# TensorE in source order in the last three blocks, the seven products of a unit in another order, and later transposes of x

## The chip, the cores and the metric

The kernel runs on one core of one Trainium2 chip. The time is that of one execution on the device, in microseconds; before the change the median of seven runs is 352.6 us (351.54 to 353.11).

## The reference

Sliding-window attention with an ALiBi bias, and then a SwiGLU feed-forward block on its result:

```python
B, H, S, D = q.shape                      # 8, 8, 576, 64; window 128
scores = scale * np.matmul(q, k.transpose(0, 1, 3, 2))
bias = slopes[:, None, None] * (-np.abs(rel))[None, :, :]
scores = np.where((rel >= 0) & (rel < window), scores + bias[None], -1000000000.0)
attn = softmax(scores)
attn_out = np.matmul(attn, v)
x = attn_out.transpose(0, 2, 1, 3).reshape(B * S, H * D)      # 4608 x 512
g = x @ w_gate                                                # 512 x 1536
return (g * sigmoid(g) * (x @ w_val)) @ w_out                 # 1536 x 512
```

Input and output are float32.

## The kernel before

Matmuls take float16 operands. Attention is cut into 36 units of 128 query rows. For a unit i, `scores(i)` makes the score products in PSUM (pool `ps_a`, four banks, tag "a"), exponentials on ScalarE and mask products on VectorE; `weighted(i)` (L344 to L347) multiplies by v on TensorE and normalises into the tile x on VectorE; `x_transposed(i)` brings x into xT, the input of the feed-forward block: by four TensorE transposes and a ScalarE copy (L370, L374) up to unit 23, by a transposing DMA on SP's queue (L365) from unit 24 on (`X_DMA_FROM`).

The feed-forward part works on nine blocks n of 512 tokens. Blocks 0 to 5 take each column of w_gate and w_val by plain 512-column matmuls (L396). Blocks 6, 7 and 8 (`gate_val_by_seven`) use Strassen's scheme (Winograd's form): 2 x 2 blocks by seven products in place of eight. A block has six units u; each of the seven products of a unit is four matmuls of 256 columns (L615) into one of three PSUM tiles: X and Y from the four banks of `ps_a`, Z from `ps_f`. Results are chained through these tiles:

- `first` starts X, and ScalarE copies X into Z (L624); `second` accumulates onto Z, then a silu on ScalarE gives s1 (L637).
- `fifth` starts Y, and ScalarE copies it to p5 (L630); `sixth` accumulates onto X, and ScalarE copies that to u2 (L644).
- `third` accumulates onto Y; VectorE adds u2 (v1, L651) and multiplies by s1 into hT (L652).
- `seventh` accumulates onto X; VectorE adds p5 (v2, L658). `fourth` accumulates onto X once more; a silu (L665) and a product on VectorE (L666) finish hT.

So each product that accumulates onto X, Y or Z has to wait for the engine that reads what was there. After the fourth product of units 3, 4 and 5 VectorE makes sums of hT (`sums`, L490 to L493) into the buffers S, of which there is one set.

The output product of a block, hT times w_out, is also done by seven products (`strassen`), once for each t in 0 and 1, so in 14 parts of six 256-column matmuls (L523), which run during the next block: `ffn` puts one part after every third product of `gate_val_by_seven`. These parts read the buffers S of their own block. After block 8 its own 14 parts follow.

What sets the order: the program is a generator for the feed-forward part (`ffn`), which counts steps, and one for attention; `everything` mixes them by a pace (`RATE`, and `ready` for the units that a block needs). This is the source order. Inside `tc.manual_schedule(engines=...)` the named engines issue in source order; that covers the first tiles up to step 8 (`ALONE`). Outside it a planner places the instructions of each engine at build time, the earlier in the source the sooner, but passing over those that by its own estimate of times are not ready. On the chip each engine's order is then fixed.

## Time and profile before

| | |
|---|---|
| median of 7 runs | 352.6 us |
| the profiled execution | 352.34 us |
| its span, first to last instruction | 350.5 us |
| TensorE busy (modelled ends) | 337.9 us, 96% |
| VectorE busy | 276.4 us, 79% |
| ScalarE busy | 205.4 us, 59% |
| GpSimd (loads) busy | 108.2 us, 31% |
| block 6 / 7 / 8 begin (first product) | 251.30 / 277.46 / 306.18 us |

A row of the timeline has the start, the duration, the engine, the line, the operation, the output and the inputs by name, the form and the number of instructions merged into it; in brackets the idle time ahead of it and what ended it. A row of the list of waits has the instruction, what it waited for, the sum, the number of times and the longest. PE is TensorE, PEld its weight loads, DVE VectorE, ACT ScalarE. The tile X of the Strassen units appears as gX, Y as gY, Z as gZ; m_reg, m_c, kT and qT are buffers of the attention part that hold sums of weights and of x in the last blocks.

## The change

From the step at which block 6 begins (198.0) TensorE issues in source order. Within a unit the order of the products, first, fifth, fourth of the unit before, second, sixth, third, seventh, becomes first, seventh of the unit before, fifth, sixth, fourth of the unit before, second, third. The transposes of x of the units 13 to 23 are put later: not right after the unit's own `weighted`, but into the third step of the scores of the second unit after it; the number of finished units that attention reports is one lower meanwhile.

```diff
--- before.py
+++ after.py
@@ -33,6 +33,8 @@
 SILU_AT = 7
 SECOND = 5.5
 RATE = 6.7
+FIXED_FROM = 198.0
+LATE = 13
 
 
 def slot(h):
@@ -645,14 +647,14 @@
             live[u] += (u2,)
 
         def third(u):
-            X, Y, Z, p5, s, u2 = live[u]
+            X, Y, Z, p5, u2, s = live[u]
             product(Y, V2, 2 * u * P, S4)
             v_ = supool.tile([P, 2, 256], FP16, name="v1", tag="uu")
             nc.vector.tensor_add(v_, Y, u2)
             nc.vector.tensor_mul(hT[n][:, 2 * u:2 * u + 2, 0:256], s, v_)
 
         def seventh(u):
-            X, Y, Z, p5, s, u2 = live[u]
+            X, Y, Z, p5, u2, s = live[u]
             product(X, tsum[u][2], 0, S3)
             v_ = supool.tile([P, 2, 256], FP16, name="v2", tag="uu")
             nc.vector.tensor_add(v_, X, p5)
@@ -667,8 +669,8 @@
 
         last_u = NMB // 2
         for u in range(last_u + 1):
-            for step, of in ((first, u), (fifth, u), (fourth, u - 1), (second, u), (sixth, u),
-                             (third, u), (seventh, u)):
+            for step, of in ((first, u), (seventh, u - 1), (fifth, u), (sixth, u), (fourth, u - 1),
+                             (second, u), (third, u)):
                 if 0 <= of < last_u:
                     step(of)
                     if step is fourth and of >= last_u // 2:
@@ -792,19 +794,29 @@
 
     def attention():
 
+        waiting = set()
         transposes_to(need[FIRST])
         for _ in run(scores(FIRST)):
             yield FIRST
         for i in range(FIRST, last + 1):
+            behind = LATE <= i < X_DMA_FROM
             if i < last:
                 transposes_to(need[i + 1])
-                for _ in run(scores(i + 1)):
-                    yield i
+                for n, _ in enumerate(run(scores(i + 1))):
+                    yield i - (i - 1 in waiting)
+                    if n == 2 and i - 1 in waiting:
+                        x_transposed(i - 1)
+                        waiting.discard(i - 1)
             weighted(i)
             yield i
             loads_to(i + 7)
             ahead(i)
             yield i
+            if behind:
+                waiting.add(i)
+                yield i
+                yield i
+                continue
             x_transposed(i)
             yield i
             yield i + 1
@@ -884,7 +896,11 @@
                     nc.scalar.copy(idm2, idm)
                 if at in (1.0, 3.0, 4.0):
                     later_masks(2 * (1, 3, 4).index(at) + 2, 2)
+        fixed = ExitStack()
         for step in steps:
+            if step >= FIXED_FROM and fixed is not None:
+                fixed.enter_context(tc.manual_schedule(engines=ENGINES["pe"]))
+                fixed, held = None, fixed
             if step == MASKS_AT:
                 make_masks()
 
@@ -902,6 +918,7 @@
                 target = base + 32 + SECOND * 8 + (step - 60) * RATE * 8 / 34.5
             while (n_att < target or done < ready[blk]) and att_step():
                 pass
+        held.close()
 
     everything()
 
```

## What I expect

> **What bounds the kernel now.** I read the page first, its busy times and its slices; then the list of waits; then the timeline of TensorE and VectorE over the last three blocks, and the one around the x transposes.

> ```profile
> PE 337.9 (96%) x2983; PEld 218.9 (62%) x2983; DVE 276.4 (79%) x652; ACT 205.4 (59%) x412; POOL 108.2 (31%) x134
> ...
> PEclk9999999999999999999999999999999999999999
> ```

> TensorE is the bound, at full clock throughout. Its 96% is not the measure, since the ends of matmuls are modelled (a 256-column one reads 273 ns); what counts is the distance from start to start. In the timeline a group of four 256-column matmuls is followed by the next after 0.437 us, a group of six after 0.655 us: 109.2 ns each, with nothing between. From the first product of block 6 (251.30 us) to the last matmul's slot (345.85 + 0.655 = 346.50) lie 95.20 us. Three blocks of 42 products of four and 14 parts of six, and 14 more parts at the end, are 3 x 252 + 84 = 840 matmuls, or 91.73 us. So TensorE loses only 3.5 us there, and that is all that an order of these instructions can win.

> The end of block 6 on TensorE:

> ```profile
> 273.97 0.82 PE L523 MATMUL po<-T,S 128*128 128x256 f16 x6
> ...
> 276.59 0.60 PE L615 MATMUL gX<-m_reg,m_c 128*128 128x256 f16 x4
> 277.02 0.60 PE L615 MATMUL gY<-m_reg,wv_sb 128*128 128x256 f16 x4
> 277.46 0.38 PE L615 MATMUL gX<-xT,wg_sb 128*128 128x256 f16 x2
> 277.86 0.60 PE L615 MATMUL gX<-m_reg,m_c 128*128 128x256 f16 x4
> 278.39 0.82 PE L523 MATMUL po<-T,hT 128*128 128x256 f16 x6
> 279.04 0.38 PE L615 MATMUL gX<-xT,wg_sb 128*128 128x256 f16 x2
> 279.26 0.60 PE L615 MATMUL gY<-xT,kT 128*128 128x256 f16 x4
> 279.70 0.82 PE L523 MATMUL po<-wo_sb,hT 128*128 128x256 f16 x6
> 280.59 0.60 PE L615 MATMUL gX<-xT,m_c 128*128 128x256 f16 x4
> ```

> From the second row on this is sixth, third, (half of the next block's first), seventh, a part of the output product, (the rest of that first, the next block's fifth, the next block's first part), fourth. The brackets are 4 + 4 + 6 = 14 matmuls, 1.53 us, pulled ahead of source order; and the fourth still starts 0.24 us after its turn. VectorE in the same stretch:

> ```profile
> 274.57 0.41 DVE L652 TENSOR_TENSOR hT<-s,v 128x512 f16<-128x512 f16 x1
> 274.90 0.42 DVE L490 TENSOR_TENSOR S<-hT 128x512 f16<-128x512 f16 x1
> ...
> 278.25 0.42 DVE L492 TENSOR_TENSOR S<-hT 128x512 f16<-128x512 f16 x1
> 278.58 0.68 DVE L651 TENSOR_TENSOR v<-gY,u 128x512 f16<-128x512 f32 x1
> 279.18 0.42 DVE L493 TENSOR_TENSOR S<-hT,S 128x512 f16<-128x512 f16 x1
> 279.52 0.42 DVE L652 TENSOR_TENSOR hT<-s,v 128x512 f16<-128x512 f16 x1
> 279.85 0.68 DVE L658 TENSOR_TENSOR v<-gX,p 128x512 f16<-128x512 f32 x1
> ```

> It runs without a pause. The sums of h (L490 to L493) write buffers that the output product of the block before still reads, so they start only when the part at 273.97 is through, and then stand ahead of what the last unit needs: its v1 (278.58), hT and v2 (L658). v2 ends at 280.53 and TensorE goes on at 280.59.

> From the waits, and the timeline around unit 15's transposes:

> ```profile
> PEld L370 <- DVE x L347: 10.2, 24, 1.0
> ```

> ```profile
> 118.40 0.59 PE L396 MATMUL pg<-xT,wg_sb 128*128 128x512 f16 x2
> 119.29 0.28 PE L370 MATMUL px<-idm,x 128*128 128x128 f16 x2 [0.30 <-DVE x L347]
> ```

> Two 512-column matmuls take 0.43 us, so the transposes could start at 118.83 and start at 119.29: 0.46 us lost because VectorE had not finished x.

> [...]

> **The change part by part.** No instruction is added or removed; all is order.

> *Order within a unit.* Now sixth to seventh has only third between, and in two units of a block no output part: the copy of X (L644, 583 ns) ends too late, and I count 0.18 us at 263.6, 277.6, 287.6, 292.4, 306.3, 320.9 and 334.9. In the new order five products lie between: gone. Newly close is first to sixth (0.87 us of products, and always one part of 0.655, since a part follows every third product): 1.53 us between them, against copy L624: 0.60 (modelled end of the group) less 0.44, plus 0.04 to 0.1 start, 0.57, 0.06 back = 0.83 to 0.9. Covered with 0.6 us, which also takes a silu (0.6) queued ahead on ScalarE. Seventh to fourth: two products and one part, 1.53 us, against v2: 0.16 + 0.1 + 0.69 + 0.06 = 1.01; 0.5 us spare for VectorE being late, as before. Fifth to third and fourth to the next first are at least as far. So the middle of a block has no wait. The two at 285.2 and 313.7 (0.35 and 0.39 us, fourth of unit 0 behind VectorE's backlog) go too if TensorE has stood still before and VectorE has caught up: worth 0.74.

> *Source order at the end of a block.* The last entries are seventh of unit 5, one part (0.655), fourth of unit 5: the new order does not change this. From the part at 273.97 to that fourth, source order holds three parts and six products, 42 matmuls, 4.59 us: due at 278.56. VectorE's work up to v2 is the same set: the sums start with the same part, at 274.90, and the shift of seventh of unit 4 by 0.44 us is hidden, because v1 and hT of that unit (0.60 + 0.33) run first. So fourth starts at 280.59 again: 2.03 us of standing still where now it is 0.24, 0.18 and a 0.10 bank wait, the rest filled. Blocks 7 and 8 give the same: 302.69 + 4.59 = 307.28 against 309.31, 331.27 + 4.59 = 335.86 against 337.89, 2.03 each. The bounds: at least 0.36 (1.45 us from the seventh's start to v2's release, 1.09 in between) if v2 meets an empty VectorE; 1.0 if three of the 0.33 us operations (a sum or two, hT) fall behind v2; at most about 2.3. I take 2.03, since VectorE was ordered alike in all three blocks and those operations stand earlier in the source. After the last block four parts (2.62 us) cover the sums of its last unit, with some 0.25 us of waits at the end.

> Sum for the blocks: 3 x 2.03 + 0.25 = 6.3 us of loss against 3.5: **+2.8 us** (bounds -2.2 and +3.7).

> *Late x transposes, units 13 to 23.* Each is moved five attention steps on, behind the score products and three exponentials of a later unit; its ScalarE copy moves with it. No DMA moves with it, and SP's transposing DMAs begin at unit 24 as before. Start to start, I count 2.0 us lost ahead of and within these eleven units' transposes, some 1.5 to 1.6 of it waiting for x (0.46, 0.28, 0.20, 0.29 and smaller ones), the rest changes between matmul forms. A delay of some 3 us covers waits of under 0.5. Against it: VectorE is 71 to 91% busy there (14.29 us of the 20 from 105 on, 18.21 of the next 20), so a TensorE that comes earlier may wait at the next product that needs it, and the planner reorders everything behind. Bounds -2.0 and +0.8; I take **-1.2**. The block that reads xT asks for finished units, so attention is only pulled ahead by up to one unit; no engine gets more work.

> Total: 352.34 (this execution; span 350.5 and 1.8 around it) + 2.8 - 1.2 = **354.0 us**. The execution lies 0.3 below the median of 352.6; I make no correction for that. What can't be told from no change is 0.2%, 0.7 us.

> **Rivals.**
> 1. *VectorE takes v2 earlier* (faster). The order of VectorE is planned anew once TensorE is fixed. With X us of standing still at each block's end the total is 3X + 0.25 - 3.5 - 1.2; it turns to a gain below X = 1.5. With three operations behind v2, X = 1.0: 351.0 us; with an empty VectorE, X = 0.36: 349.0. For it: the needed work is only 1.0 us. Against: three identical VectorE orders, with sums that precede v2 in the source.
> 2. *It cancels*: X near 1.5 or late transposes worth the full 2.0: about 352.5 us. For it: many waits on x; against: the 2.03 seen thrice.
> 3. *The late transposes win nothing or cost*: the waits for x return at the next products: 352.34 + 2.8 + 0 to 0.8 = 355.1 to 355.9. For it: VectorE's load. Against: few other TensorE waits on VectorE between units 13 and 23.
> 4. *TensorE isn't held to source order*: then the 14 matmuls still fill, and only the new order of products counts, 352.34 - 1.3 - 1.2 = 349.8. Little speaks for it.

> **Chances.** Forecast (353.3 to 355) 0.44; rival 1 0.19; rival 2 0.20; rival 3 0.14; rival 4 0.03. Slower 0.58, same 0.20, faster 0.22. The forecast's own range is 353.2 to 355.0; the range for 8 in 10 takes in half of rival 1 and most of rival 3: 350.8 to 355.4.

> **What would show it.** Right: at the end of each block seventh, six matmuls of a part, a gap near 2 us ended by v (L658), fourth; no waits of 0.18 on L644; no wait on L347 in units 13 to 23. Wrong: a gap under 1.5 us there, with L658 ahead of sums on VectorE; or new TensorE gaps between 105 and 175 us.

## The result and the profile after

The changed kernel takes 353.95 us (median of 13 runs, 353.08 to 356.65) against 352.49 (34 runs, 351.42 to 353.11) for the kernel before: ratio 1.0063, 95% interval 1.0048 to 1.0079. It is slower by 0.6%. The profiled execution is the one of 353.95 us, with a span of 352.2. (Lines from L35 on are counted two higher than before, and those of `gate_val_by_seven` likewise: L523 is now L525, L615 L617, L658 L660, L370 L372.)

The page of the kernel after, TensorE's work and clock:

```profile
PE 335.8 (95%) x2983; PEld 220.3 (63%) x2983; DVE 277.8 (79%) x652; ACT 206.9 (59%) x412; POOL 108.2 (31%) x134
...
PEclk9999999999999999999999999999999999999989
```

The instructions are as many as before on every engine. What differs is when they run, and, in one slice near the end, TensorE's granted clock, which PEclk gives in tenths of its full speed.

Where block 6 begins, on TensorE (timeline; start, duration, instruction):

```profile
247.36 1.03 PE L398 MATMUL pv<-xT,wv_sb 128*128 128x512 f16 x4
248.22 0.60 PE L617 MATMUL gX<-xT,wg_sb 128*128 128x256 f16 x4
```

That was 251.30 us: 3.1 us were won before the last blocks. From there to the end of the last matmul it took 95.20 us before; now it takes 99.88 (248.22 to 348.10): 4.7 us were lost. The difference of the two spans, 1.6 us, is these two numbers.

The wait of the weight loads for x, from the list of waits, and unit 15's transposes on the timeline:

```profile
PEld L372 <- DVE x L349: 6.3, 14, 1.0
```

```profile
120.54 0.82 PE L525 MATMUL po<-T,S 128*128 128x256 f16 x6
121.19 0.39 PE L372 MATMUL px<-idm,x 128*128 128x128 f16 x4
```

It was 10.2 us in 24 waits. The transposes follow a group of six after 0.65 us, which is exactly its time, and run without a break. Counted from start to start, the eleven units 13 to 23 lose 0.12 us around their transposes, where they lost 2.0.

The end of block 6 on TensorE:

```profile
272.68 0.82 PE L525 MATMUL po<-wo_sb,S 128*128 128x256 f16 x6
273.33 0.60 PE L617 MATMUL gZ<-xT,wg_sb 128*128 128x256 f16 x4
273.77 0.60 PE L617 MATMUL gY<-m_reg,wv_sb 128*128 128x256 f16 x4
274.20 0.60 PE L617 MATMUL gX<-m_reg,m_c 128*128 128x256 f16 x4
275.26 0.82 PE L525 MATMUL po<-T,hT 128*128 128x256 f16 x6 [0.46 <-DVE osb L529]
277.46 0.60 PE L617 MATMUL gX<-xT,m_c 128*128 128x256 f16 x4 [1.39 <-DVE v L660]
```

These are second, third, seventh, an output part and fourth, in source order, with nothing of the next block between. The part starts 1.06 us after the seventh in place of 0.437: 0.62 us lost. The fourth starts 2.20 us after the part in place of 0.655: 1.55 us lost. The bracket names a smaller time, since it counts from the modelled end of the matmul. Blocks 7 and 8 show the same two gaps to within 0.01 us (they end at 304.94 and 307.14, and at 334.61 and 336.81). VectorE beside it:

```profile
274.79 0.42 DVE L529 SCALAR_TENSOR_TENSOR osb<-po,u2s 128x256 f32<-128x256 f32 x1
275.12 0.41 DVE L494 TENSOR_TENSOR S<-hT 128x512 f16<-128x512 f16 x1
275.45 0.69 DVE L653 TENSOR_TENSOR v<-gY,u 128x512 f16<-128x512 f32 x1
276.06 0.41 DVE L495 TENSOR_TENSOR S<-hT,S 128x512 f16<-128x512 f16 x1
276.39 0.42 DVE L654 TENSOR_TENSOR hT<-s,v 128x512 f16<-128x512 f16 x1
276.73 0.68 DVE L660 TENSOR_TENSOR v<-gX,p 128x512 f16<-128x512 f32 x1
```

VectorE's operations come in the order of before. Both gaps end when VectorE is through with something: the first with the read of the output tile at 274.79 (the part writes the same PSUM tile, po), the second with v2, which ends at 277.41.

After the third gap, in block 8, the clock falls (windows; the last three columns are the granted clock, the share of the DMA engines and GB/s), and the matmuls that follow show it:

```profile
333.91:337.32 3.41, 1.57 (x14) 1.11 (x12) 2.85 (x7) 0.45 (x2) 0.00 (x0) 1.00 0.38 148
337.32:340.73 3.41, 3.41 (x18) 2.46 (x17) 1.70 (x4) 1.36 (x3) 0.00 (x0) 0.50 0.02 5
340.73:344.15 3.42, 3.42 (x33) 3.04 (x31) 1.25 (x3) 0.77 (x2) 0.00 (x0) 1.00 0.09 22
```

```profile
337.24 2.68 PE L525 MATMUL po<-wo_sb,hT 128*128 128x256 f16 x12
339.72 1.98 PE L525 MATMUL p<-wo_sb,hT 128*128 128x256 f16 x12
```

Twelve 256-column matmuls now take 2.48 us from start to start, where they took 1.31. From 337.24 to 341.53 the 24 matmuls take 4.29 us in place of 24 x 0.109 = 2.62: 1.7 us. So the 4.7 us are 3 x 2.17 = 6.5 us of gaps and 1.7 of clock, less the 3.5 us of waits that were there before; no other wait of note is left.

## The experiments

The shares of the change are tried alone first, then what makes TensorE stand still, then the clock, then how far the gain goes. Ratios are to the kernel before, run beside it on the same chip.

### Late transposes alone

The changed kernel without the fixed order and with the old order of products:

```diff
-            if step >= FIXED_FROM and fixed is not None:
-                fixed.enter_context(tc.manual_schedule(engines=ENGINES["pe"]))
-                fixed, held = None, fixed
...
-            for step, of in ((first, u), (seventh, u - 1), (fifth, u), (sixth, u), (fourth, u - 1),
-                             (second, u), (third, u)):
+            for step, of in ((first, u), (fifth, u), (fourth, u - 1), (second, u), (sixth, u),
+                             (third, u), (seventh, u)):
```

> The late transposes of x alone; TensorE is left to the planner and the products keep their old order. Theory (the waits for x are the gain, and they don't come back): block 6 begins some 3.1 us earlier, as in the changed kernel (248.2), the last blocks stay at 95.2 us, so about 349.4 us. Rival (the gain before block 6 is lent, not given: the last blocks then wait longer for VectorE): 351 to 352.5 us, with block 6 earlier and a longer rest. Only 1.2 us gained, as I had reckoned: 351.3.

Measured: 350.08 us (6 runs) against 352.35, ratio 0.9943 (0.9926 to 0.9960), so 2.0 us won, 1.4 to 2.6. In its profile block 6 begins at 248.80 and the rest takes 95.19 us, the 95.20 of before; the transposes of units 13 to 23 lose 0.12 us. The gain is kept to the end: the rival of a lent gain falls, and so does my 1.2. The 3.1 us of a single pair of profiles was too much. Up to 105 us, where the first moved transposes lie, TensorE has the same instructions in the same order in both kernels, and yet 0.67 us of the 3.1 were there by 57 us. The kernel before, then the changed one:

```profile
56.42 0.59 PE L450 MATMUL po<-wo_sb,hT 128*128 128x512 f16 x2 [0.89 <-DMA wo_sb<-in_moe_w_out_dram]
56.85 1.02 PE L396 MATMUL pg<-xT,wg_sb 128*128 128x512 f16 x4
```

```profile
55.56 0.59 PE L452 MATMUL po<-wo_sb,hT 128*128 128x512 f16 x2
56.18 1.02 PE L398 MATMUL pg<-xT,wg_sb 128*128 128x512 f16 x4
```

In one execution TensorE stood still for 1.05 us until w_out had been transferred, in the other it lost 0.19 us there. That leaves 2.4 us for the late transposes, and with them alone it is 2.4 as well (251.30 less 248.80, less 0.06 that were there before them). In the four runs below without late transposes, whose order on TensorE up to block 6 is that of before, block 6 begins anywhere from 250.3 to 252.1 us.

### Source order and new order of products, no late transposes

```diff
-LATE = 13
+LATE = 24
```

> TensorE in source order from block 6 on and the new order of products, without the late transposes. Theory (standing still at each block's end): block 6 begins at 251.3, three gaps of 2.1 to 2.2 us in all, 352.5 + 2.9 = 355.4 us, and up to 1.8 us more in executions where the clock is halved after a gap: median 355.4 to 357.2. Rival (source order costs nothing and the late transposes are what costs): 352.5 or less.

Measured: 356.43 us (6 runs, 354.78 to 358.96), ratio 1.0135 (1.0097 to 1.0174). The profile, of the execution of 354.78 us, has the clock whole up to the last matmul and takes 98.20 us from block 6 on: 3.0 more than before. The gaps are 0.62 and 1.55 us in each block. The late transposes are not what costs.

### New order of products alone

The changed kernel without the three lines that enter `manual_schedule`, and with `LATE = 24`.

> The new order of the seven products alone, TensorE left to the planner. Theory (the new order takes the seven waits of 0.18 us on the copy of X away, and the planner still pulls matmuls of the next block ahead of the fourth of unit 5): 352.5 - 1.3 = 351.2 us, no gap over 0.4 us in the last blocks. Rival (the new order by itself makes v2 late): gaps of over 1 us at the blocks' ends, 354 us or more.

Measured: 351.42 us (22 runs), ratio 0.9974 (0.9964 to 0.9984), 0.9 us faster. From block 6 on it takes 94.19 us, 1.0 less than before; no wait on the copy of X is left. I missed one thing: a gap of 0.51 us in each block ahead of the output part, ended by VectorE's read of the output tile. There is none of over 1 us.

### Source order alone

The old order of products, as in the diff of the late transposes alone, with `LATE = 24` and `manual_schedule` kept.

> TensorE in source order from block 6 on with the old order of products, no late transposes. Theory (the block's end is what source order costs, whatever the order of products): the same three gaps of some 2.1 us, and the waits of 0.18 us in units whose sixth and seventh have no output part between: 352.5 + 2.9 + 0.5 to 1.0 = 356 us, up to 1.8 more by the clock. Rival (the new order makes the gap at the end): under 354 us.

Measured: 355.55 us (6 runs, 355.18 to 356.55), ratio 1.0107 (1.0086 to 1.0128). TensorE at the end of block 6:

```profile
276.76 0.60 PE L617 MATMUL gY<-m_reg,wv_sb 128*128 128x256 f16 x4
277.60 0.60 PE L617 MATMUL gX<-m_reg,m_c 128*128 128x256 f16 x4 [0.24 <-ACT u L646]
278.13 0.81 PE L525 MATMUL po<-T,hT 128*128 128x256 f16 x6
280.33 0.60 PE L617 MATMUL gX<-xT,m_c 128*128 128x256 f16 x4 [1.39 <-DVE v L660]
```

The fourth waits 1.55 us as with the new order: the new order does not make that gap. The 0.62 us ahead of the part are only 0.09 here, but TensorE has already waited ahead of the seventh. Ahead of the seventh stands what the new order was to remove, the wait on the copy of X: 0.40 us under source order (277.60 less 276.76 less 0.437), where the planner's filling had left 0.18. It comes twice in a block. From block 6 on it takes 99.01 us, 0.8 more than with the new order.

### The sums of h asked for later

The cause named in the prediction is that VectorE's sums stand ahead of v2. Here they are only asked for later in the source; the planner then puts them behind.

```diff
-                    if step is fourth and of >= last_u // 2:
-                        sums(n, of - last_u // 2)
+                    if step is fourth and of == last_u - 1:
+                        for c in range(3):
+                            sums(n, c)
```

> The changed kernel, with the sums of h of a block asked for only after the fourth of unit 5, so that the planner puts v1 and v2 of unit 5 ahead of four of VectorE's operations. Theory (TensorE stands still because these operations are ahead of v2): v2 some 4 x 0.335 = 1.3 us earlier, the two gaps at each block's end 0.8 us together in place of 2.2, no halved clock, so about 353.3 - 3 x 1.3 = 349.4 us, a little more if the last block's sums are late for the output parts. Rival (TensorE waits for its own chain, sixth to seventh to fourth, and VectorE's queue doesn't matter): gaps as before, 353 to 354 us.

Measured: 349.22 us (6 runs, 348.95 to 349.32), ratio 0.9911 (0.9890 to 0.9931). TensorE, then VectorE, at the end of block 6:

```profile
275.29 0.60 PE L617 MATMUL gX<-m_reg,m_c 128*128 128x256 f16 x4
275.73 0.82 PE L525 MATMUL po<-T,hT 128*128 128x256 f16 x6
277.20 0.60 PE L617 MATMUL gX<-xT,m_c 128*128 128x256 f16 x4 [0.66 <-DVE v L660]
```

```profile
275.54 0.41 DVE L495 TENSOR_TENSOR S<-hT,S 128x512 f16<-128x512 f16 x1
275.87 0.68 DVE L653 TENSOR_TENSOR v<-gY,u 128x512 f16<-128x512 f32 x1
276.47 0.68 DVE L660 TENSOR_TENSOR v<-gX,p 128x512 f16<-128x512 f32 x1
277.07 0.41 DVE L654 TENSOR_TENSOR hT<-s,v 128x512 f16<-128x512 f16 x1
277.40 0.41 DVE L493 TENSOR_TENSOR hT<-hT 128x512 f16<-128x512 f16 x1
```

v2 now follows v1 at once. The gap ahead of the part is gone, and the fourth starts 1.47 us after it in place of 2.20: 0.82 us lost, all in all, in place of 2.17, in each of the three blocks. The 1.35 us are four operations of 0.335, as reckoned. So it is VectorE's queue that holds TensorE. From block 6 on it takes 94.17 us, and the last block's sums are not late for the output parts.

### Something to do in the gap

Six matmuls whose result nobody reads, ahead of the fourth of unit 5 in each block; they are work added, not a part of the computation.

```diff
+                    if step is fourth and of == last_u - 1:
+                        nil = ps_f.tile([P, 512], FP32, name="nil", tag="gv")
+                        for _ in range(6):
+                            nc.tensor.matmul(nil, wg_sb[:, 0, 0:P], wg_sb[:, 0, 0:512], start=True, stop=True)
                     step(of)
```

> The changed kernel with six 512-column matmuls of no use (1.3 us, into a PSUM buffer nobody reads) ahead of the fourth of unit 5 in each block, where TensorE stands still anyway. Theory (the halved clock after some of the gaps comes from TensorE's idleness): the fourth starts at the same time, the clock stays whole in all runs, and all runs lie where the changed kernel's runs of whole clock lie: 353.1 to 353.7 us. Rival (the halving has another cause): runs spread up to 356.6 us as in the changed kernel.

Measured: 352.76 us (14 runs, 351.94 to 353.63), ratio 1.0019 (1.0004 to 1.0033). TensorE at the end of block 6:

```profile
274.44 0.60 PE L617 MATMUL gX<-m_reg,m_c 128*128 128x256 f16 x4
275.50 0.81 PE L525 MATMUL po<-T,hT 128*128 128x256 f16 x6 [0.45 <-DVE osb L529]
276.15 1.46 PE L678 MATMUL nil<-wg_sb 128*128 128x512 f16 x6
277.70 0.60 PE L617 MATMUL gX<-xT,m_c 128*128 128x256 f16 x4
```

From seventh to fourth it is 3.26 us, as in the changed kernel (274.20 to 277.46): the added matmuls cost nothing, as the wait is set by VectorE. No run reaches 353.7 us and none has a mean clock below 0.995; the changed kernel has four runs at 355.5 to 356.7 us, with a mean clock of 0.988 or 0.989. So the halving goes when the gap is filled, and it is worth about 1.2 us of the median (353.95 against 352.76, two series of runs). In the profile of this kernel the last blocks take 98.20 us, which is the 99.88 of the changed kernel less its 1.7 us of halved clock. The runs lie half a microsecond lower than I had written. Two of them have a mean clock of 0.995 (353.28 and 353.63 us); without their traces it can't be said where in the run that was lost, and the kernel before has runs at 0.993 (352.53 us) that are no slower than some of its runs at 1.0 (352.55 to 352.69).

### Late transposes and new order, TensorE left to the planner

The change without its `manual_schedule`.

> The late transposes and the new order of products, TensorE left to the planner: the change without its fixed order. Theory: both gains and no gap: 352.5 - 3.1 - 1.3 = 348.1 us. Rival (order and late transposes gain the same microsecond): 349.4.

Measured: 349.24 us (6 runs, 347.97 to 350.56), ratio 0.9913 (0.9889 to 0.9937). That is more time than I expected, because I had taken the late transposes at the 3.1 us of the profiles; with the 2.0 and 0.9 us that the two edits won alone, 352.36 becomes 349.5. The number is the rival's, but its reason is not: from block 6 on it takes 94.18 us, where late transposes alone have 95.19, so the new order wins its 1.0 us beside them. What the planner does with the end of block 6:

```profile
273.95 0.60 PE L617 MATMUL gX<-m_reg,m_c 128*128 128x256 f16 x4
274.39 0.27 PE L617 MATMUL gX<-xT,wg_sb 128*128 128x256 f16 x1
275.00 0.82 PE L525 MATMUL po<-T,hT 128*128 128x256 f16 x6 [0.34 <-DVE osb L529]
275.65 0.49 PE L617 MATMUL gX<-xT,wg_sb 128*128 128x256 f16 x3
275.98 0.60 PE L617 MATMUL gY<-xT,kT 128*128 128x256 f16 x4
276.42 0.82 PE L525 MATMUL po<-wo_sb,hT 128*128 128x256 f16 x6
277.07 0.27 PE L617 MATMUL gX<-m_reg,kT 128*128 128x256 f16 x1
277.20 0.60 PE L617 MATMUL gX<-xT,m_c 128*128 128x256 f16 x4
```

Between seventh and fourth stand 15 matmuls of the next block (1 + 3 + 4 + 6 + 1), 1.64 us. The fourth starts 3.25 us after the seventh, as in the changed kernel, but only 0.5 us of it is lost. The 94.18 us stand against 98.2 for the same products in source order with a whole clock. That is the price of the source order: 4.0 us.

### Late transposes from unit 6 on

```diff
-LATE = 13
+LATE = 6
```

with the old order of products and no `manual_schedule`.

> The late transposes alone, from unit 6 on in place of 13. Theory (each wait for x that is covered is won): units 6 to 12 lose 2.6 us around their transposes in the kernel before, so 349.4 - 2 = 347.4 us or somewhat more. Rival (the early units are needed at once, or VectorE is the bound there, so nothing more is won): 349.4 or more.

Measured: 350.61 us (12 runs), ratio 0.9948 (0.9933 to 0.9964), no better than from unit 13 on: the rival's figure, and the theory falls. The losses around the transposes of units 6 to 12 do fall, from 2.6 to 0.9 us. One of the places where they went, in this kernel and then in the kernel before:

```profile
53.89 1.03 PE L452 MATMUL po<-wo_sb,hT 128*128 128x512 f16 x4
56.42 0.81 PE L452 MATMUL po<-wo_sb,hT 128*128 128x512 f16 x3 [1.50 <-DMA wo_sb<-in_moe_w_out_dram]
```

```profile
56.42 0.59 PE L450 MATMUL po<-wo_sb,hT 128*128 128x512 f16 x2 [0.89 <-DMA wo_sb<-in_moe_w_out_dram]
```

TensorE comes earlier to the product that needs w_out, and waits until 56.42 us as before: in these two executions the transfer is the bound there. Waits of 0.1 to 0.3 us on ScalarE's exponentials come in besides (50 to 60 us).

### The sums later, TensorE left to the planner

The edit of the sums, put on the version with late transposes and new order, and on the kernel before.

> The late transposes and the new order of products with the planner free, as in the run before, and the sums of h asked for only after the fourth of unit 5. Theory (what is left of the gaps at the blocks' ends, three of 0.51 us and one of 0.35, is VectorE's sums ahead of v2): the last blocks go from 94.2 to some 92.5 us, 349.2 - 1.5 = 347.7 us. Rival (the planner's filling has used up what the sums cost, so moving them wins nothing or makes the output parts wait for them): 349.2 us or more.

> The kernel before with nothing but the sums of h asked for later. Theory: with TensorE left to the planner the waits on v2 (0.24 three times, 0.35 and 0.39) are all that the sums cost, so at most 1.5 us are won: 350.9 to 351.8 us, against the 3 x 1.35 = 4 us that the same edit won under source order. Rival (the sums cost 4 us whatever the order of TensorE): 348.4 us.

Measured: 347.87 us (5 runs, 347.60 to 348.20), ratio 0.9887 (0.9869 to 0.9905), for the first. Its last blocks take 92.85 us; three gaps of 0.38 us are left. It beats the kernel before by 1.1% and the changed one by 1.7%. The edit alone gives 350.70 us (8 runs), ratio 0.9958 (0.9943 to 0.9973): 1.5 us, where under source order it won 4.7 (353.95 to 349.22; 4.0 of it is the last blocks at a whole clock, 98.20 to 94.17, and the clock that came back is in the rest). The late v2 costs as much as TensorE finds nothing to do meanwhile.

## Why the prediction was right

The forecast was 354.0 us and slower; 353.95 came. The mechanism that I put on the losing side is the one that the runs show, but two terms beside it were off, and they cancelled.

- *Standing still at a block's end.* Foreseen 2.03 us in each block, measured 2.17. It is in two pieces, where I expected one: the part waits 0.62 us for VectorE's read of its PSUM tile, and the fourth 1.55 us for v2. Of the wait ahead of the part I knew only the 0.10 us that it had before; the 0.25 us of waits that I expected after the last block did not come. Foreseen for the last blocks together +2.8; measured 98.20 against 95.20, +3.0, in the executions with a whole clock (source order and new order without late transposes, and the filled gap).
- *The cause.* VectorE's order was as before, and moving four operations behind v2 took 1.35 us off each block. Rival 1, a VectorE order that changes by itself, did not come; forced by hand it turned the change into a gain, as its formula says of any X below 1.5: X is 0.82 there. In size the formula has some 350.3 us, and 349.2 came; 0.8 us of the difference is what the transposes won beyond my sum, and 0.25 the waits after the last block.
- *Filling.* A late v2 costs TensorE this much only because source order forbids the planner's filling: with the same products and a free planner the last blocks take 94.2 us. So rival 4 was no case of the changed kernel, but its sum, 349.8, is close to the 349.2 of that version.
- *The new order of products.* Foreseen as 1.3 us of waits on the copy of X, gone; measured 1.0 us in the profile and 0.9 in time alone, because a gap of 0.51 us ahead of the part came in. The middle of a block has no wait, as reckoned.
- *Late transposes.* Foreseen -1.2; measured -2.0 (-2.6 to -1.4) alone. The term was too small: I expected that part of the waits for x returned at later products. The 1.9 us won around the transposes were kept to the end; new gaps did come (in the changed kernel 0.50 us up to 107.89 ahead of an output part, 0.64 us up to 171.26 within score products that wait for x), and others of the kernel before shrank, such as 0.31 us up to 163.22 on the copy p5s, now 0.17 up to 160.43.
- *The clock.* Not foreseen. I had noted a full clock throughout and never asked what a TensorE that stands still does to it. It added about 1.2 us to the median, against 0.8 us that the transposes gave beyond my sum.

With the measured terms, 352.5 - 2.0 + 3.0 + 1.2 is 354.7 us. The ratio 1.0063 of 352.5 is 354.7 as well; the median lies lower, at 353.95, as the changed kernel's runs are spread unevenly from 353.08 to 356.65 us. That it came within 0.1 us of the forecast is partly luck: a gain that I had too small and a loss that I had not foreseen nearly cancel.

## What to carry to other kernels

When an engine is the bound and hardly idle, a fixed order for it can win only the idle time that is there; before fixing it, list what the planner had pulled ahead across the seam of two stages, since that filling is what is lost. The price of the seam can be read beforehand: walk the source order with the distances from start to start, and compare with the moment at which the slower engine delivers in the trace. If the slower engine is late, change what stands in its queue ahead of the needed result first; the order of the fast engine is second.

## What the runs showed of the hardware

In the changed kernel's other runs the mean clock is 1.0 (353.08 to 353.68 us), around 0.994, or around 0.989 (355.50 to 356.65). That fits gaps that halve the clock in some executions and not in others, but a mean does not tell after which gap it happened. Source order and new order without late transposes, with the same gaps, has 0.994, 0.990 and 0.988 in three of six runs (357.46 to 358.96 us), and 0.998 to 1.0 in the others. With matmuls of no use in the gap none of 14 runs is below 0.995; what is left at the end of block 6 in its trace are gaps of 0.62 and 0.25 us. With source order alone, where 0.40, 0.09 and 1.55 us are lost there, none of six runs is below 0.998; six are too few to say that the halving can't come.
